# An mLSTM layer with top-1 experts: the last row blocks of three experts are made wider, and the group counts of the router are kept as running totals

## The chip, the cores and the metric

The kernel runs on one core of a Trainium2 chip. The metric is the time of one execution in microseconds (us) on the device, the median of several runs. TensorE does the matrix products (PE in the profile, and PEld for the loads of its stationary operand), VectorE (DVE) and ScalarE (ACT) the elementwise work, GpSimd (POOL) masks, products in SBUF and indirect transfers, and SyncE (SP) issues most transfers.

## The reference

Two parts follow each other. The first is a recurrence over 768 time steps for 4 batches and 8 heads of 40 numbers, with input, forget and output gates; its result is read as 3072 tokens of 320 numbers. The second sends every token to one of 8 experts.

```python
x = np.ascontiguousarray(attn_out.transpose(0, 2, 1, 3)).reshape(B * S, H * D)   # 3072 x 320
logits = x @ w_gate                                # 3072 x 8
expert_idx = np.argmax(logits, axis=1)
gate_w = probs[np.arange(N), expert_idx]           # probs: softmax of the logits
for e in range(E):
    mask = expert_idx == e
    h = np.maximum(x[mask] @ w1[e], 0.0)           # 320 -> 1024
    out[mask] = gate_w[mask, None] * (h @ w2[e])   # 1024 -> 320
```

How many tokens an expert gets is known only when the router has run.

## The kernel before

**First part, 24 items.** The recurrence is done in chunks of 128 steps: 6 chunks by 4 batches give 24 items of 128 tokens, and `step(s)` (L783) handles several items at different stages: `scores` (L282) and `pmul` (L289) of item s, `attend` (L305), `gated` and `state` of item s-1, `natural` (L345) and `finish` (L354) of item s-2. `finish` leaves the tokens' rows in `xs`, which `store` puts into `x_dram`, and the 8 logits of each token in `lg`. The program's order is the order of issue on every engine; no scheduler moves it.

**Routing, in 8 groups.** The items are routed in groups of 4, 4, 4, 2, 2, 4, 2 and 2 (`GROUPS`). `choose` (L383), on DVE two steps after the last item of the group, makes `oh`, a one-hot row of 8 for each token, and ends with a reduction over the group's items into `sums`, one 128x8 table a group (L401). `count` (L409), on PE one step later, adds up the place of each token in its expert's list in one PSUM tile, `pos`: a product with a triangular matrix `tri`, one product of a matrix of ones with `sums` of **each earlier group** (L415), one for each earlier item of the same group (L420), from item 14 on one with `less` and `gapb` (L425; `less` is a single row of -1, so this product has a contraction of one row), and one with the bases of the lists (L429). `place` turns this into slots, and `scatter` writes the tokens' numbers into lists in DRAM. `total` (L460) adds up `sums` over the groups so far, a product for each group, after items 12, 14 and 16 and once at the end, for the ranking of the experts.

**Second part, 10 pieces.** The experts are taken in the order of their counts, rank 0 to 7. Rank r has room for `CAPS[r]` rows, cut into blocks of at most 128 rows by `TILES[r]`; ranks 0 and 1 have 256 rows more, which are begun early as pieces a0 and a1, and their `TILES` are pieces b0 and b1. A piece has these steps: `load_list` (L545, SP) brings the list, one transfer for all blocks of the first block's size and a second for a last block that is smaller; `gather` (L561, POOL) fetches the rows, `norm` (L568, POOL) scales them; `third(k)` (L583), for the three thirds of the 320 columns, transposes each block on PE (L586: the block's rows are the contraction, so a block of 48 rows is a product with 48 rows of the array) and copies the result to SBUF on ACT and DVE. `first` (L593) multiplies with w1 for all rows of the piece at once, 8 chunks of 8 products, with ACT and DVE making `hh` and `hl` from each chunk. `second` (L612) multiplies with w2 block by block: 24 products of 320 columns a block, whose stationary operand has as many columns as the block has rows; ACT scales the result into `y`, and POOL writes the rows out by an indirect transfer (L627). The transposes of a piece stand in `second` of the piece before, `third(j)` ahead of block j. Both products use a high and a low part of weights and rows; a chunk of weights is made ready by a cast on ACT and a subtraction on DVE (`split`, L536).

`leftovers` (L637) calculates which experts have more tokens than their room; a loop at the end (L982) does them in blocks of 128. With these inputs the experts have 498, 464, 457, 422, 332, 329, 303 and 267 tokens, and no rank exceeds its room.

Of the kernel before, what the change touches and what calls it, by code (L numbers as in the profile page):

```python
# [13 lines left out]
BF16 = mybir.dt.bfloat16  # L14
# [3 lines left out]
ALU = mybir.AluOpType  # L18
AX = mybir.AxisListType

B, H, S, D = 4, 8, 768, 40
P = 128
# [8 lines left out]
E = 8  # L31
# [13 lines left out]
HEAD = HT * P  # L45
NPAIR = 2
FIRSTS = (P,) * HT
TILES = [(P,) * 2, (112,) * 2, (P, P, P, 80), (P, P, P, 48), (112,) * 3, (112,) * 3, (P, P, 64), (P, P, 32)]
CAPS = [sum(t) + HEAD * (r < NPAIR) for r, t in enumerate(TILES)]
FIRST, EARLY, MOST = 12, 14, 16  # L50
GROUPS = {
# [18 lines left out]
def mlstm_moe_kernel(ctx: ExitStack, tc: tile.TileContext, qk, og, kv, ig, fg, cst, tokid, lst0, w1, w2, out):  # L70
    nc = tc.nc
    PS = bass.MemoryType.PSUM
    const = ctx.enter_context(tc.tile_pool(name="const", bufs=1, side="left"))
# [20 lines left out]
    ones = const.tile([P, P], BF16, name="ones")  # L94
# [3 lines left out]
    oh = const.tile([P, NITEM, E], BF16, name="oh")  # L98
    sums = const.tile([P, len(GROUPS), E], BF16, name="sums")
# [4 lines left out]
    top = const.tile([P, 2, E], F32, name="top")  # L104
    big = const.tile([P, E], F32, name="big")
    gapb = const.tile([P, E], BF16, name="gapb")
    less = const.tile([1, P], BF16, name="less")
    ls0, ls1 = (const.tile([P, HT, 3], F32, name=f"ls{k}") for k in range(2))
    xg0, xg1 = (const.tile([P, HT, XR], F32, name=f"xg{k}") for k in range(2))
    xh0 = const.tile([P, 3, HEAD], F32R, name="xh0")  # L110
# [29 lines left out]
    at = list(spare)  # L140
# [239 lines left out]
    starts = [i0 for i0, _ in GROUPS.values()]  # L380
    group_of = starts.index

    def choose(i0, n):  # L383

        l3 = lg[:, i0 : i0 + n, :]
        b8 = lambda t: t.unsqueeze(2).to_broadcast([P, n, E])
        mx = mx_ps[:, :n]
        yield nc.vector.tensor_reduce(mx, l3, axis=AX.X, op=ALU.max)
        d = d_ps[:, : n * E].rearrange("p (n e) -> p n e", e=E)
        yield nc.vector.tensor_tensor(d, l3, b8(mx), ALU.subtract)  # L390
        rt["d", i0] = d

        sc = sm.tile([P, n, E], F32, name=f"sc{i0}", tag="sc")
        yield nc.vector.scalar_tensor_tensor(
            sc, d, 0.0, rev.unsqueeze(1).to_broadcast([P, n, E]), ALU.is_equal, ALU.mult
        )
        m2 = m2_ps[:, :n]
        yield nc.vector.tensor_reduce(m2, sc, axis=AX.X, op=ALU.max)
        yield nc.vector.tensor_tensor(oh[:, i0 : i0 + n, :], sc, b8(m2), ALU.is_equal)
        with nc.allow_low_precision("counts of at most four"):  # L400
            yield nc.vector.tensor_reduce(  # L401
                sums[:, group_of(i0)], oh[:, i0 : i0 + n, :].rearrange("p n e -> p e n"), axis=AX.X, op=ALU.add
            )

    def weights_of(i0, n):
# [3 lines left out]
    def count(i0, n):  # L409

        o3 = oh[:, i0 : i0 + n, :]
        rt["pos", i0] = pos = pos_ps[:, : n * E].rearrange("p (n e) -> p n e", e=E)
        nc.tensor.matmul(pos, tri, o3, start=True, stop=False, skip_group_check=True)
        for g in range(group_of(i0)):
            nc.tensor.matmul(  # L415
                pos, ones, sums[:, g].unsqueeze(1).to_broadcast([P, n, E]), start=False, stop=False,
                skip_group_check=True,
            )
        for j in range(n - 1):
            nc.tensor.matmul(  # L420
                pos[:, j + 1 :], ones, oh[:, i0 + j].unsqueeze(1).to_broadcast([P, n - 1 - j, E]), start=False,
                stop=False, skip_group_check=True,
            )
        if i0 >= EARLY:
            nc.tensor.matmul(  # L425
                pos, less, gapb[0:1].unsqueeze(1).to_broadcast([1, n, E]), start=False, stop=False,
                skip_group_check=True,
            )
        nc.tensor.matmul(pos, ones, baseb[:, :n], start=False, stop=True, skip_group_check=True)  # L429
# [30 lines left out]
    def total(items):  # L460

        rt["pc", items] = pc = pc_ps
        n = sum(i0 < items for i0 in starts)
        for g in range(n):
            nc.tensor.matmul(pc, ones, sums[:, g], start=g == 0, stop=g == n - 1)

    def rank(k, items):

# [225 lines left out]
    def start():  # L694
# [12 lines left out]
        for t, a, b in ((keep, 1.0, 0.0), (drop, 0.0, -1e30)):  # L707
# [3 lines left out]
        nc.gpsimd.affine_select(  # L711
            tri, ones, pattern=[[1, P]], compare_op=ALU.is_gt, fill=0.0, base=0, channel_multiplier=-1
        )
        nc.gpsimd.memset(less, -1.0)
        nc.gpsimd.memset(gapb, 0.0)
        nc.gpsimd.memset(zrow, 0.0)
        stir(8)
# [65 lines left out]
    def step(s):  # L783
# [44 lines left out]
        if chosen:  # L828
            weave(choose(*chosen))
# [36 lines left out]
    _, third = transpose_x("a0", xg0, FIRSTS)  # L866
    with tc.manual_schedule():
        start()
        for s in range(NITEM + 1):
            if s == 14:  # L870
# [21 lines left out]
        pieces = [(f"a{r}", r, 0, FIRSTS) for r in range(NPAIR)]  # L892
        pieces += [(f"b{r}", r, HEAD, TILES[r]) for r in range(NPAIR)]
        pieces += [(str(r), r, 0, TILES[r]) for r in range(NPAIR, E)]
        ls = {"a0": ls0, "a1": ls1}
# [6 lines left out]
        store(NITEM - 2)  # L902
        weave(finish(NITEM - 1))
        weave(choose(NITEM - 2, 2))
        weights_of(NITEM - 2, 2)
        store(NITEM - 1)
# [75 lines left out]
    with tc.For_i(0, nu) as u:  # L982
        e = nc.sync.value_load(tab[:, 0, ds(u, 1)], min_val=0, max_val=E - 1)
        at = nc.sync.value_load(tab[:, 1, ds(u, 1)], min_val=0, max_val=E * SS - P)
# [88 lines left out]
```

## Time and profile before

| | |
|---|---|
| median of 3 runs | 350.41 us (348.66, 350.41, 350.65) |
| profiled execution | 348.27 us, span 346.7 us |
| PE busy | 332.2 us (96%), 3370 products |
| DVE, ACT, POOL busy | 218.3, 190.6, 180.7 us |
| mean granted clock of TensorE | 0.975 |
| first part, with its routing | 0 to about 133 us |
| pieces a0 to b1 | about 133 to 202 us |
| ranks 2 to 7 | about 189 to 341.5 us |

The time of an execution is 1.6 us over its span. Products on PE overlap in their pipeline, so a row's duration is the time that one product takes from start to end (about 0.3 us), and the distance from one start to the next is what it costs in a dense stretch; a busy share of 96% therefore hides waits of less than about 0.2 us. The granted clock is 1.00 when TensorE has its full clock and 0.50 when it has half.

### The profile page before, as it was taken

To read this page: it belongs to the slowest core of one execution; us is meant where nothing else is said; L and a number is where in the kernel's file an instruction comes from. 1 tells how busy PE (TensorE), PEld (TensorE's weight loads), DVE (VectorE), ACT (ScalarE), POOL (GpSimd) and SP (SyncE) were. 2 spreads that over 40 slices of the span, in tenths; PEclk is the share of its full clock that TensorE was granted. 3 is DMA by queue.
4 is the path that set the end of the run, shared out by engine and by line. 5 is a ranking of instruction groups with operands and counts; after the bars stand their busy time and mean duration, and the time that the engine had idled before them with its cause. 6 is when DMAs were issued, how large, how long until landed. Compare 5 with 4: busy or idle time off the path is not lost. (4 is left out here: it accounts for less than half of the span.)

```text
span 346.7 us, 9329 instructions
## 1 busy us (share of the span) xinstructions
PE 332.2 (96%) x3370; PEld 307.7 (89%) x3370; DVE 218.3 (63%) x591; ACT 190.6 (55%) x477; POOL 180.7 (52%) x222
## 2 busy tenths in 40 slices
PE   7998999999999989998999999999999999999994
PEld 3797888999888768997999988999999999999992
DVE  5997888789789977854224758428427446374310
ACT  3989786777688732552325645336427445374311
POOL 7666597978986983317546661244145262222112
PEclk9899999999999965999999999999999999999999
DMA  6888888785989985548521874633654747630000
GB/s 168 254 253 243 265 229 202 210 234 140 247 196 233 275 183 140 153 48 250 155 70 42 254 190 115 206 115 110 194 146 120 205 130 219 172 92 22 27 19 23
DMA packets 33409, 56.75 MB, mean 164 GB/s; under 512 B 6296, under 2 KB 21437, under 8 KB 33346
## 3 DMA queue, kind: packets, MB, share of 16 engines
q1 hardware_dynamic: 29746, 47.88, 51.2%
q0 software_dynamic: 3424, 8.14, 7.8%
q8 instruction: 27, 0.44, 0.6%
q14 instruction: 20, 0.16, 0.2%
q10 hardware_dynamic: 192, 0.12, 0.1%
HBM read 48.12 MB, written 8.47 MB: 163 GB/s over the span
## 5 line engine op out<-in xcount | busy, mean ns | idle before, releaser
L622 PE MATMUL py<-w2h,hh 128*128 128x320 f32 (+5 forms) x224 | 71.3, 318 | 0.0
L622 PE MATMUL py<-w2h,hl 128*128 128x320 f32 (+5 forms) x224 | 69.0, 308 | 0.0
L622 PE MATMUL py<-w2l,hh 128*128 128x320 f32 (+5 forms) x224 | 69.0, 308 | 0.0
L627 POOL DMA_INDIRECT out<-y,ls x20 | 19.5, 973 | 94.6 <-ACT xh L587 57.9
L248 ACT ACTIVATE dd<-bc_ps,aT 128x128 f32<-128x128 f32 x184 | 51.0, 395 | 1.6 <-PE bc_ps L229 1.6
L607 DVE SCALAR_TENSOR_TENSOR hl<-bc_ps,hh 128x256 fp32r<-128x256 f32 (+6 forms) x54 | 25.6, 480 | 28.8 <-ACT hh L606 24.8
L622 PEld LDWEIGHTS py<-w2h,hh 128*128 128x128 f32 (+5 forms) x224 | 39.3, 176 | 1.0
L622 PEld LDWEIGHTS py<-w2l,hh 128*128 128x128 f32 (+5 forms) x224 | 39.3, 176 | 0.5
L622 PEld LDWEIGHTS py<-w2h,hl 128*128 128x128 f32 (+5 forms) x224 | 39.2, 175 | 0.6
L606 ACT ACTIVATE hh<-bc_ps 128x256 fp32r<-128x256 f32 (+6 forms) x54 | 23.4, 434 | 28.4 <-PE bc_ps L599 25.5
L626 ACT ACTIVATE y<-py,ls 128x320 f32<-128x320 f32 (+5 forms) x20 | 10.6, 528 | 49.6 <-issue 38.0
L257 POOL TENSOR_SCALAR_AFFINE_SELECT dd<-dd 128x1024 f32<-128x1024 f32 (+1 forms) x25 | 28.0, 1119 | 17.7 <-ACT dd L248 13.4
L599 PE MATMUL bc_ps<-xh,w1h 128*128 128x336 f32 (+5 forms) x114 | 36.7, 329 | 0.0
L599 PE MATMUL bc_ps<-xh,w1l 128*128 128x336 f32 (+5 forms) x114 | 36.4, 326 | 0.0
L534 DVE TENSOR_TENSOR w1l<-raw,w1h 128x1024 fp32r<-128x1024 f32 x24 | 30.7, 1280 | 6.9 <-ACT w1h L530 6.2
L452 POOL DMA_INDIRECT lst<-rec,slot x24 | 26.0, 1081 | 13.3 <-DVE r L362 4.3
L293 DVE TENSOR_TENSOR pp<-s_ps,dd 128x512 f32<-128x512 f32 x48 | 30.7, 679 | 0.3 <-issue 0.2
L287 PE MATMUL s_ps<-tq 40*128 40x128 f32 x384 | 29.7, 288 | 1.2 <-DVE pp L293 1.1
L563 POOL DMA_INDIRECT xg<-x_dram,ls x24 | 26.1, 1086 | 8.9 <-issue 5.2
L534 DVE TENSOR_TENSOR w2l<-raw,w2h 128x640 fp32r<-128x640 f32 x32 | 25.8, 821 | 7.5 <-ACT w2h L530 6.7
L349 PE MATMUL x_ps<-cs,yT 105*128 105x98 f32 x184 | 28.1, 298 | 2.6 <-ACT ex L407 1.9
L287 PEld LDWEIGHTS s_ps<-tq 40*128 40x128 f32 x384 | 24.5, 189 | 4.2 <-DVE pp L293 1.9
(223 smaller groups left out, 783.9 us busy)
## 6 DMA issues: line engine op xcount, KB each, us to landing
raw<-in_w SPq DMA_DIRECT2D x32, 320.0 KB
raw<-in_w SPq DMA_DIRECT2D x16, 512.0 KB
tk<-in_kv SPq DMA_DIRECT2D x24, 324.0 KB
tq<-in_qk SPq DMA_DIRECT2D x48, 160.0 KB
raw<-in_w SPq DMA_DIRECT2D x16, 256.0 KB
x_dram<-xs SPq DMA_DIRECT2D x24, 164.0 KB
og<-in_og SPq DMA_DIRECT2D x48, 80.0 KB
lst<-rec,slot POOLq DMA_INDIRECT x24
```

The lines of the kernel that those rows point to most:

```text
L248: nc.scalar.activation(dd[:, h, :], bc_ps[h // 4][:, (h % 4) * P : (h % 4 + 1) * P], AF.Exp, bias=aT[:, c, i : i + 1], scale=-1.0,)
L257: nc.gpsimd.affine_select(part, part, pattern=[[0, n], [1, P]], compare_op=ALU.is_ge, fill=0.0, base=0, channel_multiplier=-1)
L287: nc.tensor.matmul(s_ps[h // 4][:, p * P : (p + 1) * P], k, q, start=True, stop=True)
L293: nc.vector.tensor_mul(pp[:, 4 * k : 4 * k + 4], s_ps[k].rearrange("p (h t) -> p h t", t=P), t["dd"][:, 4 * k : 4 * k + 4])
L349: nc.tensor.matmul(x[:, o], t["yT"][:, o * P : (o + 1) * P], cs[:OR, C_R + o * XW : C_R + (o + 1) * XW], start=True, stop=True,)
L452: ins = nc.gpsimd.indirect_dma_start(out=lst, out_offset=bass.IndirectOffsetOnAxis(ap=slot[:, it : it + 1], axis=0), in_=rec[:, it, :], in ...
L534: nc.vector.tensor_sub(w[name + "l"][:, c], t, f32(w[name + "h"][:, c]))
L563: nc.gpsimd.indirect_dma_start(out=xg[:t, j], out_offset=None, in_=x_dram[: 1 + items * P], in_offset=bass.IndirectOffsetOnAxis(ap=ls[:t, ...
L599: nc.tensor.matmul(ph[:, :n], a[:, k, fs], b[:, k, :n], start=i == 0, stop=i == len(terms) - 1)
L606: nc.scalar.activation(hh[:, f, :n], ph[f][:, :n], AF.Relu)
L607: nc.vector.scalar_tensor_tensor(hl[:, f, :n], ph[f][:, :n], 0.0, f32(hh[:, f, :n]), ALU.max, ALU.subtract)
L622: nc.tensor.matmul(py[:t], a[:, f, ts], b[:, f], start=(f == 0 and i == 0), stop=(f == NF - 1 and i == 2))
```

## The change

Three of the rows of `TILES` are cut differently, with the same sums: rank 3 from (128, 128, 128, 48) to (112, 112, 112, 96), rank 6 from (128, 128, 64) to (112, 112, 96), rank 7 from (128, 128, 32) to (96, 96, 96). All three keep their number of blocks. `sums` of a group becomes the count over all items so far, so that `count` needs one product with `sums` of the group before and `total` one product in all; the reduction on DVE reads all items so far instead of the group's own. `less` becomes a full 128x128 matrix whose first row is -1 and whose others are 0, and is multiplied with all 128 rows of `gapb`.

```diff
-TILES = [(P,) * 2, (112,) * 2, (P, P, P, 80), (P, P, P, 48), (112,) * 3, (112,) * 3, (P, P, 64), (P, P, 32)]
+TILES = [
+    (P,) * 2, (112,) * 2, (P, P, P, 80), (112, 112, 112, 96), (112,) * 3, (112,) * 3, (112, 112, 96), (96,) * 3
+]
...
-    less = const.tile([1, P], BF16, name="less")
+    less = const.tile([P, P], BF16, name="less")
...
             yield nc.vector.tensor_reduce(
-                sums[:, group_of(i0)], oh[:, i0 : i0 + n, :].rearrange("p n e -> p e n"), axis=AX.X, op=ALU.add
+                sums[:, group_of(i0)], oh[:, : i0 + n, :].rearrange("p n e -> p e n"), axis=AX.X, op=ALU.add
             )
...
-        for g in range(group_of(i0)):
+        if i0:
+            before = sums[:, group_of(i0) - 1]
             nc.tensor.matmul(
-                pos, ones, sums[:, g].unsqueeze(1).to_broadcast([P, n, E]), start=False, stop=False,
-                skip_group_check=True,
+                pos, ones, before.unsqueeze(1).to_broadcast([P, n, E]), start=False, stop=False, skip_group_check=True
             )
...
-                pos, less, gapb[0:1].unsqueeze(1).to_broadcast([1, n, E]), start=False, stop=False,
+                pos, less, gapb.unsqueeze(1).to_broadcast([P, n, E]), start=False, stop=False,
...
-        n = sum(i0 < items for i0 in starts)
-        for g in range(n):
-            nc.tensor.matmul(pc, ones, sums[:, g], start=g == 0, stop=g == n - 1)
+        nc.tensor.matmul(pc, ones, sums[:, sum(i0 < items for i0 in starts) - 1], start=True, stop=True)
...
-        nc.gpsimd.memset(less, -1.0)
+        nc.gpsimd.memset(less, 0.0)
+        nc.gpsimd.memset(less[0:1], -1.0)
```

On PE, `count` and `total` of step 18 (items 14 and 15) stand like this before (a `LDWEIGHTS` row loads the stationary operand of the product behind it, and 128x16 is the product's output):

```order
L415 LDWEIGHTS ones
L415 MATMUL x_ps<-sums,ones 128x16
...
L420 LDWEIGHTS ones
L420 MATMUL x_ps<-oh,ones 128x8
L425 LDWEIGHTS less
L425 MATMUL x_ps<-gapb,less 128x16
L429 LDWEIGHTS ones
L429 MATMUL x_ps<-baseb,ones 128x16
L465 LDWEIGHTS ones
L465 MATMUL x_ps<-sums,ones 128x8
...
```

and like this in the change (line numbers are two or three higher):

```order
L418 LDWEIGHTS ones
L418 MATMUL x_ps<-sums,ones 128x16
L422 LDWEIGHTS ones
L422 MATMUL x_ps<-oh,ones 128x8
L427 LDWEIGHTS less
L427 MATMUL x_ps<-gapb,less 128x16
L431 LDWEIGHTS ones
L431 MATMUL x_ps<-baseb,ones 128x16
L465 LDWEIGHTS ones
L465 MATMUL x_ps<-sums,ones 128x8
```

Of four products at L415 one is left, and of five at L465 one. Over the program 21 and 16 products go, with their loads.

On PE, the transposes of rank 7 in `second` of rank 6, ahead of its first block, before:

```order
L599 MATMUL g_ps<-xh_4326,w1l_1528 128x320
L586 MATMUL s_ps_131<-cs,xg_4328 128x128 x2
L586 MATMUL s_ps_131<-cs,xg_4328 128x32
L622 MATMUL py_2693<-w2h_1529,hh 128x320
L622 MATMUL py_2693<-w2l_1530,hh 128x320
```

and in the change:

```order
L599 MATMUL g_ps<-xh_4289,w1l_1529 128x320
L586 MATMUL s_ps_131<-cs,xg_4291 128x96 x3
L622 MATMUL py_2670<-w2h_1530,hh 112x320
L622 MATMUL py_2670<-w2l_1531,hh 112x320
L622 MATMUL py_2670<-w2h_1530,hl 112x320
```

The number of transposes and products stays; their rows and the blocks' rows change. On SP the list of rank 7 was two transfers and is one, so that the weight transfers behind it stand one place further ahead:

```order
L552 DMA ls_2852<-lst 128x6
L552 ISA
L552 DMA ls_2852<-lst 32x3
L525 ISA
L525 DMA raw_2958<-in_w 128x1024
```

has become

```order
L552 DMA ls_2823<-lst 96x9
L525 ISA
L525 DMA raw_2928<-in_w 128x1024
```

where `raw` is the buffer into which a chunk of weights is loaded. Nothing else of SP's order moves.

## Rows read from the trace of the kernel before

**Rows 1.** Busy time by stretch (`PEclk`: granted clock); bounds in us from the span's start.
```profile
120.80:124.20 3.40, 3.40 (x22) 2.77 (x18) 3.17 (x4) 0.72 (x1) 2.94 (x4) 0.50 0.97 231
127.60:137.90 10.30, 9.81 (x52) 9.27 (x53) 7.19 (x29) 3.41 (x9) 5.50 (x10) 0.50 0.62 129
189.00:341.50 152.50, 152.11 (x999) 145.34 (x998) 79.78 (x138) 71.27 (x131) 51.30 (x54) 1.00 0.47 134
```

**Rows 2.** Waits of PE from 138 to 346 us: total, times, longest.
```profile
PE s_ps L586 <- POOL xgb L571: 0.6, 2, 0.3
```

**Rows 3.** Timeline of PE: transposes of a third, and the product behind them.
```profile
195.48 0.56 PE L586 MATMUL s_ps<-cs,xg 128*128 128x128 f32 x4
195.83 0.38 PE L622 MATMUL py<-w2h,hh 128*112 128x320 f32 x1
...
218.02 0.68 PE L586 MATMUL s_ps<-cs,xg 128*128 128x128 f32 x4
218.63 0.42 PE L622 MATMUL py<-w2h,hh 128*128 128x320 f32 x1
...
250.01 0.45 PE L586 MATMUL x_ps<-cs,xg 112*64 112x112 f32 x3
250.23 0.39 PE L622 MATMUL py<-w2h,hh 128*128 128x320 f32 x1
...
292.50 0.58 PE L586 MATMUL s_ps<-cs,xg 128*128 128x128 f32 x3
293.01 0.40 PE L622 MATMUL py<-w2h,hh 128*112 128x320 f32 x1
...
318.32 0.53 PE L586 MATMUL x_ps<-cs,xg 128*64 128x128 f32 x3
318.77 0.36 PE L622 MATMUL py<-w2h,hh 128*64 128x320 f32 x1
```

**Rows 4.** Timeline of PE's loads: the fourth transpose at 218 us.
```profile
218.44 0.14 PEld L586 LDWEIGHTS s_ps<-cs,xg 48*128 48x128 f32 x1 [0.17 <-issue]
```

**Rows 5.** Timeline of PE: the end of a count, and the last total.
```profile
97.30 0.17 PE L420 MATMUL x_ps<-oh,ones 128*128 128x8 bf16 x1
...
97.51 0.18 PE L429 MATMUL x_ps<-baseb,ones 128*128 128x16 bf16 x1
...
201.56 0.36 PE L465 MATMUL x_ps<-sums,ones 128*128 128x8 bf16 x8
201.77 0.46 PE L599 MATMUL bc_ps<-xh,w1h 128*128 128x464 f32 x1
```

**Rows 6.** DVE by line and form: the reduction into `sums`.
```profile
L401 DVE TENSOR_REDUCE sums<-oh 128x8 bf16<-128x32 bf16 x4 | 0.8, 206 | 0.1
L401 DVE TENSOR_REDUCE sums<-oh 128x8 bf16<-128x16 bf16 x4 | 0.7, 171 | 0.1
```

**Rows 7.** Timeline of DVE: the wait for it that ends at 118.1 us.
```profile
115.36 0.21 DVE L401 TENSOR_REDUCE sums<-oh 128x8 bf16<-128x32 bf16 x1
...
117.36 1.27 DVE L293 TENSOR_TENSOR pp<-s_ps,dd 128x512 f32<-128x512 f32 x2
```

**Rows 8.** Timeline of PE at that wait.
```profile
118.10 1.75 PE L287 MATMUL s_ps<-tq 40*128 40x128 f32 x16 [0.53 <-DVE pp L293]
```

**Rows 9.** Waits of PE from 20 to 133 us: those of scores for `pp`.
```profile
PE s_ps L287 <- DVE pp L293: 0.5, 1, 0.5
```

**Rows 10.** PE and PEld by line and form: products and loads of `second`.
```profile
L622 PE MATMUL py<-w2h,hl 128*128 128x320 f32 x128 | 39.4, 308 | 0.0
L622 PE MATMUL py<-w2h,hl 128*32 128x320 f32 x8 | 2.4, 306 | 0.0
...
L622 PEld LDWEIGHTS py<-w2h,hl 128*128 128x128 f32 x128 | 24.0, 188 | 0.0
L622 PEld LDWEIGHTS py<-w2h,hl 128*32 128x32 f32 x8 | 0.9, 108 | 0.3
```

**Rows 11.** The transfers out by tile: duration in ns, least, median, most.
```profile
L627 POOL DMA_INDIRECT out<-y,ls x20: 879/984/1033, 219.3 to 343.4; - x20
```

More of the change, by code (lines that the diff above doesn't have):

```diff
@@ L399, in choose @@
         yield nc.vector.tensor_tensor(oh[:, i0 : i0 + n, :], sc, b8(m2), ALU.is_equal)
-        with nc.allow_low_precision("counts of at most four"):
+        with nc.allow_low_precision("counts of at most 24"):
             yield nc.vector.tensor_reduce(
-                sums[:, group_of(i0)], oh[:, i0 : i0 + n, :].rearrange("p n e -> p e n"), axis=AX.X, op=ALU.add
+                sums[:, group_of(i0)], oh[:, : i0 + n, :].rearrange("p n e -> p e n"), axis=AX.X, op=ALU.add
             )
```

## The prediction

> **What bounds the kernel now.** I read the busy time by stretch first, then the waits of TensorE (PE), then its timeline where the change acts. From 189 us to 341.5 us PE is busy for 152.11 of 152.50 us at a granted clock of 1.00 [rows 1], and from 138 us to the end its longest kind of wait is 0.6 us, two pieces of 0.3 us, both for POOL's scaled rows at 160 us [rows 2]. So in ranks 2 to 7 the distance from one PE instruction to the next is the time itself, and what is taken out there moves the end. Ahead of 133 us it is mixed: PE waits now and then for DVE or ACT, as for 0.53 us at 118.10 us, for DVE's `pp` [rows 8]. Between 120.8 and 137.9 us the clock is at 0.50 for 3.4 and then 10.3 us [rows 1].
>
> **The transposes.** Rank 2 is cut into 128, 128, 128 and 80 rows, and its four transposes take 0.35 us from the first of them to the product behind them (195.48 to 195.83). Three of 112 rows take 0.22 us (250.01 to 250.23). Rank 3, with a last block of 48, takes 0.61 us (218.02 to 218.63); rank 6, with 64, takes 0.51 us (292.50 to 293.01); rank 7, with 32, takes 0.45 us in its last third (318.32 to 318.77) [rows 3]. The row of the loads shows where it goes: the load for the 48-row transpose, unlike those around it, begins only after 0.17 us in which nothing is loaded [rows 4], so it waits for the products in flight, and the product behind it then has to wait again. A block of 80 doesn't do this, so 96 and 112 shouldn't.
> There are three thirds a rank, hence nine such groups. Before: 3 x 0.61 + 3 x 0.51 + 3 x 0.45 = 4.71 us. After, by columns: rank 3 has 432 columns of transposes where rank 2 has 464, 0.35 x 432/464 = 0.33 us; rank 6 has 320 where three of 112 have 336, 0.21 us; rank 7 has 288, 0.19 us. That is 3 x (0.33 + 0.21 + 0.19) = 2.19 us. Saved: **2.5 us**, all of it between 213 and 319 us, in the stretch that has no waits. Least 0 (if the stop belonged to something else), most 2.8 us, if the stop also costs in the first product behind it.
> The 112x64 group at 250.01 us is one of third 2, where the output is only 64 rows wide, and it costs no more than 0.22 us [rows 3]: the stop comes from few rows of contraction, not from few columns. The Trainium skill, TensorEngine Tiling (Array Packing), section Key Properties, says that a change of the tiling mode drains the engine, and its Tiling Modes count 64 columns as a mode of their own. By that the three groups of third 2 would keep their stop and the saving would be about 1.7 us; the trace agrees for 48 and 64 rows and differs for 64 columns.
>
> **Products with wider blocks.** The last blocks go from 48, 64 and 32 columns of the stationary operand to 96. A product with 32 takes 306 ns and one with 128 takes 308 ns [rows 10]: 72 products x 2 ns = **+0.1 us**.
>
> **The end.** The last block written out has 96 rows and not 32. POOL's instruction takes between 0.88 us and 1.03 us over all sizes [rows 11], so at most +0.15 us; the transfer's own time for three times the rows stands in no row, and I bound it from 0 to 0.45 us, three times that spread. I take **+0.3 us** for both.
>
> **The counts.** Eight products with `sums` take 0.21 us (201.56 to 201.77), 0.026 us each. The product with `less` is different: from the product ahead of it to the one behind it pass 0.21 us (97.30 to 97.51) [rows 5], where two steps of the others make 0.05; with 128 rows it saves 0.16 us, four times. Removed products, by place: 3 in step 14, 5 in step 16, 7 in step 18 (with `less`), 4 in step 22 (with `less`), 5 in step 24 (with `less`), 6 in piece a0 (with `less`), 7 in the last total.
> Step 22's is lost: it stands right ahead of the wait at 118.10 us, which grows by what PE is early. Piece a0's is lost too: PE then waits at 160 us for rows that come through DVE and POOL [rows 2], which are no earlier. On the path remain 3 + 5 + 7 + 5 + 7 = 27 products x 0.026 = 0.70 us and 2 x 0.16 = 0.32 us: **-1.0 us**. At least 0.2 us (the last total alone, if the steps wait elsewhere), at most 1.6 us (37 x 0.026 + 4 x 0.16).
>
> **The longer reduction on DVE.** It reads 32, 64, 96, 112, 128, 160, 176 and 192 numbers where it read 32 or 16. From 16 to 32 it grows from 171 to 206 ns [rows 6], 2.2 ns a number, so the eight get longer by 0, 0.07, 0.14, 0.21, 0.25, 0.28, 0.35 and 0.39 us. Those up to step 17 delay a `pp` that stands behind them on DVE, but in the whole first part PE's scores wait for `pp` once only, at 118 us [rows 9]; without that cover they would cost 0.67 us. Step 23's lies ahead of an idle time of DVE, and a0's likewise; without these, 0.74 us. Step 21's is bare: at 115.36 us it stands ahead of a weight chunk and of the `pp` at 117.36 us [rows 7], for which PE waits at 118.10 us [rows 8]. **+0.3 us**, from 0 to 1.7 us.
>
> **What I put at nothing.** The second memset of `less` (one of 128 rows and one of one row, for one before) lies on POOL ahead of its first mask, which waits for ACT. One list transfer fewer lets the weight transfers behind it on SP start earlier; PE waits for no weights in these rows, and it would matter only if they were late. POOL's gathers and scalings keep their number and their columns.
>
> **Sum.** -2.5 + 0.1 + 0.3 - 1.0 + 0.3 = **-2.8 us**. Against the profiled execution: 348.27 - 2.8 = 345.5 us. The median shown is 350.41 us, 2.1 us above that execution; one of its runs lies at 348.66 and two at 350.4 to 350.7. With the median as the base: **347.6 us**.
>
> **Rivals.**
> (a) Only part of it arrives: third 2 keeps its stop, or the steps before 113 us give nothing because they end on ACT and DVE. For it speaks that PE waits there for others in some steps; against it the 112x64 group, and that its scores wait once only [rows 9]. Gain 0.8 to 2.0 us, 348.4 to 349.6 us. Chance 0.17.
> (b) The clock, which ends slower. PE's wait at 118.10 us grows to 0.53 + 0.26 + 0.28 = 1.07 us, just ahead of the stretch at 0.50 from 120.8 us [rows 1]. Each further 3.4 us at half clock of dense products loses 1.7 us. One leaves a gain of 1.1 us; from the second on the change loses, 2 x 1.7 - 2.8 = +0.6 us, 351.0 us; four give 354.4 us. Against it: behind 137.9 us PE has its products back to back, and from 189 us the clock stays at 1.00 [rows 1]. One: chance 0.05; two or more: 0.04.
> (c) The clock the other way: with the shifted steps a half-clock stretch of 3.4 us is missing, a further -1.7 us, 345.9 us or less. Nothing in the rows favours it over (b) but its order of size. Chance 0.06.
> (d) The wider loads show. A load of 32 columns takes 108 ns and one of 128 takes 188 ns [rows 10], 0.83 ns a column; 24 loads x 144 columns more x 0.83 = 2.9 us, which would eat all of the transposes' gain: 350.5 us. Against it: the products with 128 columns, whose loads are longer than any of the new ones, take 308 ns like those with 32 take 306. The Trainium skill, TensorE: Matmul & The Clock Gate, section LDWEIGHTS, has a load's time grow with its columns and not with its rows, which speaks against this change; the trace agrees on the load and shows it hidden. Chance 0.02.
> (e) The change doesn't do what it says: blocks of 96 or 112 stop as well, so that only the counts remain, 350.0 us. The 80-row block speaks against it. Chance 0.02.
> The forecast itself, a gain of 2.0 to 3.6 us: 0.64.
>
> **How the numbers follow.** The forecast's own range is 346.8 to 348.4 us on the median's base. An execution like the profiled one would lie 2.1 us lower, at 344.7 to 346.3 us, and two of the four times shown are of that kind; so the range starts at 345.2 us. Upward it takes in (a) and ends at 349.6 us; outside remain most of (b), (d), (e) and a low execution with the full gain, together under 0.2. A measurement of this kernel tells about 1% from no change, 3.5 us. Faster by that means under 346.9 us: the forecast's range straddles that bound once the lower executions are counted, and I give it half of 0.64 less a little, 0.31; with (c) 0.37. Slower by over 1% is (b) from some four stretches on; I leave it the whole 0.04. Within 1%: 0.59.
>
> **What would show it.** Each of the nine groups of transposes in ranks 3, 6 and 7 at 0.19 to 0.36 us; no load with 0.17 us of idle time before it there. Counts with products 0.026 us apart through `less`. The reduction at 0.4 to 0.56 us in the last groups, and PE's wait near 118 us at about 1 us. From 213 to 319 us the stretch shorter by 2.5 us, and the tail behind the last product longer by 0.3 us. The prediction is wrong if these hold and the time doesn't follow, which would put the loss into 97 to 160 us, or if a group with 96 rows takes over 0.4 us.

## The result, and the profile after

The changed kernel takes 345.94 us (median of 6 runs, 345.02 to 348.10), the kernel before beside it 350.48 us (6 runs, 348.66 to 351.10): a ratio of 0.9885, 95% interval 0.9848 to 0.9922. Two later comparisons gave 0.9869 (0.9832 to 0.9905; 345.35 against 349.08 us) and 0.9954 (0.9910 to 0.9997; 345.06 against 347.62 us). The three differences of the medians are 4.5, 3.7 and 2.6 us; the prediction had 2.8 us. The medians are over all executions and the ratios leave out those that ran long, so the one does not divide into the other; by the ratios the gains are 4.0, 4.6 and 1.6 us.

The profiled execution of the changed kernel is the slowest of its six (348.10 us), that of the kernel before (348.27 us) is faster than every one of the six that stand beside the changed kernel. The two spans, 346.5 and 346.7 us, therefore don't show the difference; it has to be looked for stretch by stretch. In the stretch in which PE is busy throughout, by the columns of [rows 1]:

```profile
189.00:341.50 152.50, 151.43 (x1011) 148.41 (x1009) 81.20 (x139) 73.42 (x136) 52.61 (x56) 1.00 0.47 134
```

The granted clock is 1.00 and PE is busy for 151.43 of 152.50 us; the end of that window now reaches into the tail. The first transpose of rank 2 starts at 193.63 us, the last product of all at 340.48 us: 146.85 us, where before they were at 191.53 and 341.15 us, 149.62 us. So 2.77 us have gone between two points with the same work between them.

The timeline of PE, a third of ranks 3, 6 and 7 each as in [rows 3], the third one being third 2 with its 64-row output:

```profile
215.72 0.54 PE L586 MATMUL s_ps<-cs,xg 112*128 112x112 f32 x4
216.04 0.39 PE L622 MATMUL py<-w2h,hh 128*128 128x320 f32 x1
...
223.56 0.54 PE L586 MATMUL x_ps<-cs,xg 112*64 112x112 f32 x4
223.88 0.39 PE L622 MATMUL py<-w2h,hh 128*128 128x320 f32 x1
...
289.38 0.44 PE L586 MATMUL s_ps<-cs,xg 112*128 112x112 f32 x3
289.60 0.39 PE L622 MATMUL py<-w2h,hh 128*112 128x320 f32 x1
...
317.77 0.41 PE L586 MATMUL x_ps<-cs,xg 96*64 96x96 f32 x3
317.97 0.36 PE L622 MATMUL py<-w2h,hh 128*96 128x320 f32 x1
```

From the first transpose to the product behind it: 0.32 us three times in rank 3, 0.22 us three times in rank 6, 0.19 to 0.20 us three times in rank 7, 2.21 us in all. Before, the nine were 0.60, 0.61, 0.58, 0.51, 0.51, 0.49, 0.49, 0.49 and 0.45 us, 4.73 us: **2.52 us less**. And the loads of rank 3's transposes are one row without a gap, where [rows 4] had 0.17 us ahead of the fourth:

```profile
215.51 0.55 PEld L586 LDWEIGHTS s_ps<-cs,xg 112*128 112x128 f32 x4
216.01 0.19 PEld L622 LDWEIGHTS py<-w2h,hh 128*128 128x128 f32 x1
```

The last total is one product now, and the next product of `first` starts 0.03 us behind it instead of 0.21 us [rows 5]:

```profile
203.66 0.18 PE L465 MATMUL x_ps<-sums,ones 128*128 128x8 bf16 x1
203.69 0.45 PE L599 MATMUL bc_ps<-xh,w1h 128*128 128x464 f32 x1
```

That is 0.18 us, and with the transposes 2.70 of the 2.77 us.

The count of step 22, and the scores of step 23 behind it: the product with `less` (L427) takes its place in the pitch of 0.03 us, without the stop that [rows 5] showed, and PE then waits for `pp` as in [rows 8]:

```profile
119.33 0.22 PE L422 MATMUL x_ps<-oh,ones 128*128 128x24 bf16 x3
119.40 0.18 PE L427 MATMUL x_ps<-gapb,less 128*128 128x32 bf16 x1
119.43 0.18 PE L431 MATMUL x_ps<-baseb,ones 128*128 128x32 bf16 x1
120.27 0.48 PE L289 MATMUL s_ps<-tq 40*128 40x128 f32 x2 [0.67 <-DVE pp L295]
```

On DVE, the longer reduction with 160 and with 192 numbers, where [rows 6] had 171 and 206 ns for the group's own:

```profile
118.05 0.43 DVE L403 TENSOR_REDUCE sums<-oh 128x8 bf16<-128x160 bf16 x1
118.40 1.21 DVE L534 TENSOR_TENSOR w1l<-raw,w1h 128x1024 fp32r<-128x1024 f32 x1
119.54 1.28 DVE L295 TENSOR_TENSOR pp<-s_ps,dd 128x512 f32<-128x512 f32 x2
...
137.98 0.49 DVE L403 TENSOR_REDUCE sums<-oh 128x8 bf16<-128x192 bf16 x1
```

A wait that had not been there shows in the view of PE's waits from 138 to 346 us. Before, the longest single one in that view was of 0.6 us, the first of these lines, which [rows 2] doesn't have; the others are those of the changed kernel:

```profile
PE bc_ps L599 <- issue: 0.6, 1, 0.6
...
PE bc_ps L599 <- DVE sums L403: 2.2, 1, 2.2
PE bc_ps L599 <- issue: 0.8, 1, 0.8
PE bc_ps L599 <- DVE hl L607: 0.4, 1, 0.4
```

Piece a0's products ran at full clock here and came to the end of the chain of choices on DVE, which the reduction at 137.98 us closes, before DVE did. The wait ends at 138.96 us, and from 140.5 us the granted clock is 0.50 for 3.4 us, in dense products:

```profile
140.50:143.90 3.40, 3.40 (x22) 3.31 (x21) 2.01 (x6) 0.79 (x4) 0.72 (x1) 0.50 0.45 100
```

Two further profiles of the same kernel ("again" and "once more" below) have half clock ahead of this place, from 130.5 us on, and don't have this wait.

The end: POOL's instruction for the last transfer out, which took 0.88 us at 343.43 us before.

```profile
342.85 0.92 POOL L627 DMA_INDIRECT out<-y,ls  x1 [3.54 <-issue]
```

From the last product's start to POOL's instruction 2.37 us (before 341.15 to 343.43, 2.28 us), from there to the end of the span 3.63 us (before 3.23 us): the tail is 6.0 us and was 5.5 us.

What hides all this in the two spans lies in front. The scores of step 3 (the fourth of 24; the expectations below call them those of step 4, and those of step 23, the last, those of step 24):

```profile
21.91 1.16 PE L289 MATMUL s_ps<-tq 40*128 40x128 f32 x16
```

In the profiled execution before they started at 20.00 us. The half clock of the start lay at 17.6 to 21.0 us here and at 11.6 to 15.0 us there. The kernel before, profiled once more (last experiment), had these scores at 22.7 us, behind half clock from 11.1 to 21.4 us: the difference goes with the execution, not with the change.

### The profile page after: what moved, and what is told of

Same layout as the page of the kernel before. It is cut to its first block, busy times and chain, and to the rows that moved or that the text cites. A ratio compares the mean times of both kernels' runs of the same rounds, so it can differ in the third digit from the quotient of the medians.

```text
span 346.5 us, 9253 instructions
## 1 busy us (share of the span) xinstructions
PE 327.5 (95%) x3333; PEld 305.4 (88%) x3333; DVE 219.3 (63%) x591; ACT 189.9 (55%) x477; POOL 178.7 (52%) x223
## 5 line engine op out<-in xcount | busy, mean ns | idle before, releaser
L622 PE MATMUL py<-w2h,hh 128*112 128x320 f32 (+3 forms) x224 | 71.1, 317 | 0.0
L622 PE MATMUL py<-w2h,hl 128*112 128x320 f32 (+3 forms) x224 | 69.1, 308 | 0.0
L622 PE MATMUL py<-w2l,hh 128*112 128x320 f32 (+3 forms) x224 | 69.1, 308 | 0.0
L622 PEld LDWEIGHTS py<-w2l,hh 128*112 128x112 f32 (+3 forms) x224 | 39.3, 176 | 0.0
L622 PEld LDWEIGHTS py<-w2h,hh 128*112 128x112 f32 (+3 forms) x224 | 39.3, 175 | 0.0
L622 PEld LDWEIGHTS py<-w2h,hl 128*112 128x112 f32 (+3 forms) x224 | 39.2, 175 | 0.0
L259 POOL TENSOR_SCALAR_AFFINE_SELECT dd<-dd 128x1024 f32<-128x1024 f32 (+1 forms) x25 | 26.8, 1073 | 21.5 <-ACT dd L250 13.3
L626 ACT ACTIVATE y<-py,ls 112x320 f32<-112x320 f32 (+3 forms) x20 | 10.5, 527 | 47.2 <-issue 35.8
L534 DVE TENSOR_TENSOR w1l<-raw,w1h 128x1024 fp32r<-128x1024 f32 x24 | 29.5, 1231 | 7.3 <-ACT w1h L530 7.2
```

Of the source, the lines that this page charges most:

```text
L259: nc.gpsimd.affine_select(part, part, pattern=[[0, n], [1, P]], compare_op=ALU.is_ge, fill=0.0, base=0, channel_multiplier=-1)
L534: nc.vector.tensor_sub(w[name + "l"][:, c], t, f32(w[name + "h"][:, c]))
L622: nc.tensor.matmul(py[:t], a[:, f, ts], b[:, f], start=(f == 0 and i == 0), stop=(f == NF - 1 and i == 2))
```

## The experiments

My theory: PE stops where a transpose contracts over 64 rows or fewer, these nine stops are the gain, and what the counts save is small. Against it: the counts and `less`, which free PE in the part with the routing, are most of it; that the stop belongs to something else than the rows; and that the longer reduction gives the counts' gain back.

**The cut of the ranks alone.**

```diff
-TILES = [(P,) * 2, (112,) * 2, (P, P, P, 80), (P, P, P, 48), (112,) * 3, (112,) * 3, (P, P, 64), (P, P, 32)]
+TILES = [
+    (P,) * 2, (112,) * 2, (P, P, P, 80), (112, 112, 112, 96), (112,) * 3, (112,) * 3, (112, 112, 96), (96,) * 3
+]
```

> The kernel before with the new block sizes alone. Theory A (the stop at transposes of 64 rows or fewer): the nine groups of transposes in ranks 3, 6 and 7 at 0.19 to 0.33 us, 2.6 us less in all, the tail 0.3 to 0.5 us longer, so 2.2 us faster than before. Theory B (most of the 4.5 us comes from the counts): the groups shrink, but the time falls by under 1.5 us.

Measured 346.21 us against 349.08 us, ratio 0.9893 (0.9854 to 0.9932). Groups of 0.32, 0.22 and 0.19 us; rank 2's transposes to the last product 147.0 us, tail 6.0 us. That is 2.9 us by the medians, where 2.2 us were expected; the cut alone brings most of the change.

**The running totals alone**, `less` left with one row.

```diff
-                sums[:, group_of(i0)], oh[:, i0 : i0 + n, :].rearrange("p n e -> p e n"), axis=AX.X, op=ALU.add
+                sums[:, group_of(i0)], oh[:, : i0 + n, :].rearrange("p n e -> p e n"), axis=AX.X, op=ALU.add
...
-        for g in range(group_of(i0)):
+        if i0:
...
```

> The kernel before with the running totals alone; the row of -1 keeps its one row. Theory A: 37 products fewer, 0.7 us of them on the path, the longer reductions cost 0.3 us, so 0.4 us faster (0 to 1). Theory B: 2 us or more faster, from the first part up to 160 us.

Measured 348.01 us, ratio 0.9964 (0.9931 to 0.9997). Transposes as before; rank 2's transposes to the last product 149.4 us, so 0.2 us less, the last total. The interval allows from 0.1 to 2.4 us, which excludes neither expectation.

**The full `less` alone.**

```diff
-    less = const.tile([1, P], BF16, name="less")
+    less = const.tile([P, P], BF16, name="less")
...
-                pos, less, gapb[0:1].unsqueeze(1).to_broadcast([1, n, E]), start=False, stop=False,
+                pos, less, gapb.unsqueeze(1).to_broadcast([P, n, E]), start=False, stop=False,
```

> The kernel before with the full matrix in place of the row of -1 alone. Theory A: four products follow the one before them after 0.03 us and not 0.10 us, two of them on the path, so 0.3 us faster (0 to 0.6). Theory B: 1 us or more faster, since the first part waits less behind it.

Measured 348.75 us, ratio 0.9978 (0.9952 to 1.0005): it can't be told from no change, though a gain of up to 1.7 us is not excluded. 149.6 us from rank 2's transposes to the last product.

**The changed kernel again**, beside these three.

> The changed kernel once more, for a second profile and beside the parts. Theory A: 4 to 5 us faster than before as measured, with the transposes' stretch 2.7 us shorter as in the first profile and the rest gained ahead of 190 us, where the first profile had lost 2 us by 22 us from the start. Theory B: the same time, with the gain ahead of 190 us larger than the one behind it.

Measured 345.35 us, ratio 0.9869: 3.7 us by the medians, a little under the expected 4 to 5 us. The three parts add up to 1.07 + 0.36 + 0.22 = 1.65% against 1.31% for the whole, each to some 0.35%: they add up as far as can be told. The profile (345.18 us) has the same kind of start as the first one of before (scores of step 3 at 20.0 us) and is 3.1 us shorter than that, with 146.85 us behind rank 2's first transposes.

**Last blocks of 72 rows.** Is it the bound at 64, or something finer?

```diff
-TILES = [
-    (P,) * 2, (112,) * 2, (P, P, P, 80), (112, 112, 112, 96), (112,) * 3, (112,) * 3, (112, 112, 96), (96,) * 3
-]
+TILES = [(P,) * 2, (112,) * 2, (P, P, P, 80), (120, 120, 120, 72), (112,) * 3, (112,) * 3, (124, 124, 72), (108, 108, 72)]
```

> The changed kernel with the last blocks of ranks 3, 6 and 7 at 72 rows (120, 120, 120, 72; 124, 124, 72; 108, 108, 72) in place of 96. Theory A (only blocks of 64 rows or fewer stop TensorE): the nine groups of transposes take 0.20 to 0.33 us each, 2.2 us in all, and the time is that of the changed kernel within 0.3%. Rival (rows that are no multiple of 16 or 32 stop it as well, or the bound lies above 72): groups of 0.45 to 0.6 us, 4.7 us in all, and a time about 2.4 us longer than the changed kernel's.

The groups take 0.34, 0.24 and 0.22 us, 2.39 us in all (some 0.02 us each over the changed kernel's), and rank 2's transposes to the last product 147.0 us. No stop at 72 rows, though 72, 108, 120 and 124 are no multiples of 16. Measured 344.85 us against 347.56 us, ratio 0.9930 (0.9874 to 0.9986), within the spread of the changed kernel's three ratios; the changed kernel was not timed beside it. Here is rank 6's third 0:

```profile
284.02 0.44 PE L584 MATMUL s_ps<-cs,xg 124*128 124x124 f32 x3
284.26 0.38 PE L620 MATMUL py<-w2h,hh 128*112 128x320 f32 x1
```

**The old blocks, with 128 rows of contraction.** The blocks of 48, 64 and 32 rows come back, but are turned by a product with the identity's first columns over all 128 rows, the rows beyond the block zeroed by POOL.

```diff
-                nc.tensor.transpose(pt[:r, at : at + t], xg[:t, j, k * P : k * P + r], ident[:t, :t])
+                if t > 64:
+                    nc.tensor.transpose(pt[:r, at : at + t], xg[:t, j, k * P : k * P + r], ident[:t, :t])
+                else:
+                    nc.tensor.matmul(
+                        pt[:r, at : at + t], xg[:, j, k * P : k * P + r], ident[:, :t], start=True, stop=True
+                    )
...
+                if t <= 64:
+                    nc.gpsimd.memset(xg[key][t // 64 * 64 :, j, :DM], 0.0)
```

> The changed kernel with the old blocks of 48, 64 and 32 rows, but each of these transposed by a product over all 128 rows of contraction (rows beyond the block are zeroed, the right operand is the identity's first 48, 64 or 32 columns). Theory A (the stop comes from few rows of contraction): no stop, the nine groups take 0.20 to 0.36 us each, 2.3 us in all, and the tail behind the last product is 5.5 us and not 6.0: 0.3 to 0.6 us faster than the changed kernel. Rival (the stop comes from the narrow output, 32 to 64 columns): the groups keep 0.45 to 0.6 us, 4.7 us in all, and the time is about 2 us longer than the changed kernel's.

Measured 346.93 us against 347.56 us, ratio 0.9982 (0.9931 to 1.0034), an interval too wide to decide between the two expectations. The profile (an execution of 356.56 us) shows that neither holds as it stands; its clock is at 1.00 in the rows below. First rank 3's third 0, its loads and then its products (L587 is the new one; in single precision it comes as two):

```profile
222.57 0.46 PEld L585 LDWEIGHTS s_ps<-cs,xg 128*128 128x128 f32 x3
223.00 0.30 PEld L587 LDWEIGHTS s_ps<-cs,xg 128*128 128x128 f32 x2
223.22 0.19 PEld L625 LDWEIGHTS py<-w2h,hh 128*128 128x128 f32 x1
```

```profile
222.78 0.49 PE L585 MATMUL s_ps<-cs,xg 128*128 128x128 f32 x3
223.11 0.32 PE L587 MATMUL s_ps<-cs,xg 128*128 128x48 f32 x2
223.25 0.39 PE L625 MATMUL py<-w2h,hh 128*128 128x320 f32 x1
```

No gap in the loads, and 0.47 us for the group (0.36 us in ranks 6 and 7): with the same 48 columns of output, and 128 rows, the stop is gone, in thirds 0 and 1 of all three ranks. What remains over the changed kernel's 0.32 us goes with the two loads of 128 columns for one block. In rank 3's third 2, whose stationary operand has 64 columns, the stop is there again:

```profile
230.78 0.36 PEld L585 LDWEIGHTS x_ps<-cs,xg 128*64 128x64 f32 x3
231.34 0.19 PEld L587 LDWEIGHTS x_ps<-cs,xg 128*64 128x64 f32 x2 [0.20 <-issue]
231.58 0.19 PEld L625 LDWEIGHTS py<-w2h,hh 128*128 128x128 f32 x1
```

0.66, 0.57 and 0.54 us for these three groups. The nine sum to 4.15 us, nearer to the rival's 4.7 than to the theory's 2.3: 0.58 us are saved where the cut saves 2.52, and the tail is the old one, 5.5 us. I had not thought of third 2 as a case of its own. (This profile has half clock from 16.0 to 29.7 and from 36.5 to 50.1 us, and no time is read from its first part.)

**The short reduction, with the total added on POOL.**

```diff
-                sums[:, group_of(i0)], oh[:, : i0 + n, :].rearrange("p n e -> p e n"), axis=AX.X, op=ALU.add
+                sums[:, group_of(i0)], oh[:, i0 : i0 + n, :].rearrange("p n e -> p e n"), axis=AX.X, op=ALU.add
...
+    def running(i0, n):
+        if i0:
+            own = sums[:, group_of(i0)]
+            with nc.allow_low_precision("counts of at most 24"):
+                nc.gpsimd.tensor_add(own, own, sums[:, group_of(i0) - 1])
...
```

> The changed kernel with the reduction on DVE cut back to the group's own rows (16 or 32 numbers, 0.17 to 0.21 us) and the total of the groups before added by POOL at the end of the step. Theory (the longer reduction is what eats the counts' gain): PE's wait for pp at 118 to 120 us goes from 0.67 to 0.4 us or less, piece a0's wait for sums gets shorter by 0.3 us if POOL's addition lies aside, and the time is 0.3 to 0.7 us shorter than the changed kernel's. Rival (the counts' gain is lost because the steps end on ACT and DVE anyhow): the step starts from 30 to 118 us stay where they are within 0.3 us and the time is the changed kernel's within 0.1%.

Both expectations fell: 352.19 us against 347.56 us, ratio 1.0178 (1.0091 to 1.0265). The addition takes 0.2 us on POOL but stands behind its masks and list transfers, and PE waits for it:

```profile
PE x_ps L471 <- POOL sums L411: 2.6, 3, 1.4
```

The longest, 1.40 us, ends at 100.57 us, and the granted clock is 0.50 from 102.0 to 115.7 us, a place where no other profile has half clock:

```profile
102.00:115.70 13.70, 13.70 (x146) 11.89 (x142) 8.49 (x31) 6.86 (x20) 9.00 (x12) 0.50 0.89 245
```

13.7 us of dense products at half clock lose some 6.8 us, by an estimate from this row; the scores of step 23 come 94.5 us behind those of step 5, 5 to 9 us later than in the table below. The stretch behind rank 2's transposes is the changed kernel's, 146.8 us. So what the prediction's rival (b) feared, half clock soon behind a wait, does occur in this kernel. The changed kernel itself has it too: in its first profile half clock begins at 140.5 us, 1.5 us behind the end of the wait of 2.22 us, and in the profile "once more" below at 116.9 us, inside a wait of 3.09 us. It does not always follow: in the profiles with the full `less` alone and with the cut alone waits of 2.38 and 1.52 us, which end at 161.64 and 160.04 us, have no half clock behind them.

**Each reduction twice.** If the longer reduction were what eats the counts' gain, doubling it would show.

```diff
-            yield nc.vector.tensor_reduce(
-                sums[:, group_of(i0)], oh[:, : i0 + n, :].rearrange("p n e -> p e n"), axis=AX.X, op=ALU.add
-            )
+            for _ in range(2):
+                yield nc.vector.tensor_reduce(
+                    sums[:, group_of(i0)], oh[:, : i0 + n, :].rearrange("p n e -> p e n"), axis=AX.X, op=ALU.add
+                )
```

> The changed kernel with each reduction into the totals of the groups done twice in a row on DVE (the same values): 0.20 + 0.27 + 0.33 + 0.36 + 0.38 + 0.43 + 0.47 + 0.49 = 2.9 us more of DVE. Theory (DVE's time in the first part is covered but for step 21's and piece a0's reductions): PE's wait for pp at 118 to 120 us grows from 0.67 to about 1.1 us, piece a0 starts up to 0.5 us later, and the time is 0.4 to 1.0 us longer than the changed kernel's. Rival (DVE's time is the bound of steps 14 to 24, and the longer reduction is what ate the counts' gain): the scores of step 24 come 2 us later or more, seen from those of step 5, and the time is 2 to 3 us longer.

Measured 346.37 us, ratio 0.9942 (0.9898 to 0.9987), beside the changed kernel's 345.06 us, 0.9954 (0.9910 to 0.9997). From the scores of step 5 to those of step 23 it needs 87.2 us, no more than the others (table below), and the wait at 118 us is

```profile
118.39 1.75 PE L289 MATMUL s_ps<-tq 40*128 40x128 f32 x16 [0.80 <-DVE pp L295]
```

0.80 us and not 1.1. The median is 1.3 us over the changed kernel's and the ratio 0.1% below its own, so 2.9 us more on DVE cost nothing that can be told; the rival, whose scores would come 2 us later, fell.

**The change without its running totals** (the new cut, the full `less`, a product for each group and the short reduction).

Against the kernel before:

```diff
-TILES = [(P,) * 2, (112,) * 2, (P, P, P, 80), (P, P, P, 48), (112,) * 3, (112,) * 3, (P, P, 64), (P, P, 32)]
+TILES = [
+    (P,) * 2, (112,) * 2, (P, P, P, 80), (112, 112, 112, 96), (112,) * 3, (112,) * 3, (112, 112, 96), (96,) * 3
+]
...
-                pos, less, gapb[0:1].unsqueeze(1).to_broadcast([1, n, E]), start=False, stop=False,
+                pos, less, gapb.unsqueeze(1).to_broadcast([P, n, E]), start=False, stop=False,
...
```

> The kernel before with the new cut of the ranks and the less operand of 128 rows, but a product for each group and the short reduction: the change without its running totals. If the running totals give what the prediction's terms give (34 products of 0.026 us of which 27 lie on the path, against 0.3 us of DVE), it is 0.4 us slower than the changed kernel; if the longer reduction costs more than the products, it is faster by up to 1 us. By the sum of the parts measured so far 0.3% slower.

Measured 345.37 us, ratio 0.9952 (0.9917 to 0.9987): 0.3 us over the changed kernel, less than can be told. Rank 2's transposes to the last product 147.0 us.

**The changed kernel once more**, on the same chip as the last two.

> The changed kernel again, on the same chip as the two others, to compare them with: a ratio to the kernel before of 0.985 to 0.992.

0.9954 is above the expected 0.985 to 0.992, and the upper end of its interval, 0.9997, all but reaches no change. The gain in the time is known only as 0.5 to 1.3%. Its profile (342.92 us) has a wait that shows what the first part waits for:

```profile
117.56 0.79 PE L289 MATMUL s_ps<-tq 40*128 40x128 f32 x2 [3.09 <-DVE pp L295]
```

```profile
112.71 0.45 DVE L403 TENSOR_REDUCE sums<-oh 128x8 bf16<-128x160 bf16 x1
113.07 3.83 DVE L534 TENSOR_TENSOR w1l<-raw,w1h 128x1024 fp32r<-128x1024 f32 x1
116.83 1.27 DVE L295 TENSOR_TENSOR pp<-s_ps,dd 128x512 f32<-128x512 f32 x2
```

PE had come to this place early: the last product of the count starts 84.9 us behind step 5's scores (114.29 - 29.4), in the first profile of this kernel 87.8 us (119.43 - 31.6). 2.9 us had been gained on the way, and the wait is 2.4 us longer. The weight chunk ahead of `pp` stood on DVE for 3.83 us. The chunks are cast on ACT and subtracted on DVE in the same order, and the cast of this one had run from 108.87 to 109.98 us, so it was not waiting for that. What lies beside it are products of two operands on POOL (L271 and L571; the masks of L259 have one):

```profile
112.88 1.27 POOL L271 TENSOR_TENSOR qg<-tq,gb 104x512 f32<-104x512 f32 x1
...
115.76 2.40 POOL L571 TENSOR_TENSOR xg<-xg 128x320 f32<-128x320 f32 x2
```

The same place in the first profile of the kernel before, where such a product of POOL runs until 116.35 us:

```profile
115.48 1.96 DVE L534 TENSOR_TENSOR w1l<-raw,w1h 128x1024 fp32r<-128x1024 f32 x1
```

All profiles but the padded kernel's show it for the three chunks of `w1l` from 102 to 130 us: 1.21 to 1.28 us where at most 0.2 us of a chunk lies beside such a product, 1.3 to 1.6 us beside 0.24 to 0.56 us, 2.0 to 2.1 us beside 0.87 to 1.05 us, and 3.83 us here, beside 2.22 us. That the product on POOL is what holds DVE up fits all of them; no run here varies it by itself.

**The kernel before, profiled once more.**

> The kernel before, once more, for a second profiled execution: scores of step 4 at 20.0 us or at 21.6 to 21.9 us from the span's start, whichever of the two kinds of start it has; if the later one, the span is 1.6 to 1.9 us longer than the first profiled execution's, and the stretch from rank 2's first transposes to the last product's start is 149.6 us either way.

349.13 us (one execution), span 347.5 us, scores of step 3 at 22.7 us (neither of the two values I had named), and 149.6 us between the two points. Its time is 0.9 us over the first profile's though it starts 2.7 us later, so the start does not decide alone either.

The profiles, in us from their timelines (the half clock is the time at a granted clock of 0.50 from 113 to 189 us). The padded and the POOL kernel, with half clock between 30 and 113 us, are not among them:

| profile | step 5's scores | to step 23's | to rank 2's transposes | to the last product | tail | half clock |
|---|---|---|---|---|---|---|
| before | 29.7 | 88.4 | 73.4 | 149.6 | 5.5 | 13.7 |
| before, once more | 32.5 | 86.9 | 73.1 | 149.6 | 5.5 | 10.2 |
| full `less` | 31.3 | 88.3 | 73.9 | 149.6 | 5.5 | 17.1 |
| running totals | 31.4 | 88.3 | 73.5 | 149.4 | 5.5 | 13.7 |
| cut alone | 29.7 | 89.1 | 73.1 | 147.0 | 6.0 | 10.2 |
| cut and `less` | 31.2 | 86.0 | 74.7 | 147.0 | 6.0 | 20.5 |
| after | 31.6 | 88.6 | 73.4 | 146.8 | 6.0 | 6.8 |
| after, again | 29.7 | 88.2 | 72.8 | 146.8 | 6.0 | 10.2 |
| after, once more | 29.4 | 88.2 | 70.8 | 146.9 | 6.0 | 10.2 |
| 72 rows | 31.3 | 85.9 | 71.1 | 147.0 | 6.0 | 13.7 |
| reduction twice | 31.2 | 87.2 | 73.5 | 146.9 | 6.0 | 13.7 |

The two columns behind rank 2 are the same to 0.2 us in every execution of a kind. Those ahead of it spread by 2.8 and 2.6 us over four executions that run almost the same instructions there: "72 rows" differs from "after", "after, again" and "after, once more" only from the list of rank 3 on, which SP loads behind 150 us.

## Why the prediction was right, and where it was not

The forecast of -2.8 us lies inside the three measured differences of 2.6 to 4.5 us, and 345.94 us inside its own range. What the profiles can place is -2.5 us for the transposes, -0.2 us for the last total and +0.5 us for the tail, -2.2 us in all; what the medians show beyond that isn't placed. That the forecast lies among the measured differences is in part luck: it has 0.8 us more gain from the counts than the profiles place, and the measured gain holds something that neither the forecast nor the profiles place. By its steps:

- **Transposes, -2.5 us: right**, in size (-2.52 us) and in mechanism. No stop at 72 rows or more, stops at 48, 64 and 32; the same 48, 64 and 32 columns of output with 128 rows of contraction don't stop where 128 columns are loaded. So for transposes few rows of contraction make it, as the prediction read it from the 80-row block [rows 3].
- **64 columns.** The prediction weighed a sentence of the Trainium skill, TensorEngine Tiling (Array Packing), Key Properties, that a change of the tiling mode drains the engine, against the 112x64 group, and took the row. For transposes the runs bear that out: third 2 of ranks 3, 6 and 7 takes 0.32, 0.22 and 0.20 us. But the product over 128 rows with 64 columns, in the padded kernel, does stop by 0.20 us. That stop fits the sentence of the Trainium skill only if the transposes with 64 columns right ahead of it are not in the mode for 64 columns, since from one product with 64 columns to the next no mode would change. The products of `second` with 48 and 32 columns of the kernel before do not stop either: they follow those with 128 at 0.14 us (253.68 to 253.82 us, 337.71 to 337.85 us). The runs leave open what parts these three; the padded product is the only one that shows as two products.
- **Wider blocks, +0.1 us: nothing seen.** 309 ns for a product with 96 columns, 306 ns with 32 [rows 10], but the distance from one to the next, which is what counts here, is 0.15 us with either. The longer loads of the last blocks stay hidden, 161 ns in place of 108. Rival (d) had a fault of its own: its 2.9 us counted the 144 columns that the last blocks gain and not the 144 that the other blocks lose (3 x 16, 2 x 16 and 2 x 32), so that at 0.83 ns a column it comes to nothing even if no load is hidden.
- **The end, +0.3 us: too small by 0.2 us**, inside its bounds. 0.13 of the 0.5 us lie ahead of the last transfer's issue and in it, the rest in the transfer.
- **The counts, -1.0 us: mis-sized; the profiles place 0.2 us of it.** The rows came as said: no stop at `less`, a pitch of 0.03 us. The last total gave 0.18 us. The step that failed is the claim that 27 of the products remain on the path, which rested on PE's scores waiting for `pp` only once [rows 9]. The steps wait for more than `pp`: in the profile after, from 20 to 133 us, PE waits 1.3 us for `yT`, 0.7 us for DVE's L485 and 0.6 us for ACT's exponentials, and these waits come and go between executions of the same instructions. What the counts free in a step is within that; the running totals and `less` alone show 0.4% and 0.2%, with intervals that reach to 0.03% and beyond nothing. Against the change without its running totals the whole change gains 0.3 us by the medians and nothing by the ratios. A gain of the predicted size can't be excluded by these runs; it isn't shown either.
- **The longer reduction, +0.3 us: nearer to nothing.** It takes 0.20 to 0.49 us, 1.8 ns a number and not 2.2. The wait at 118 us was said to become 1.07 us; in the changed kernel it was 0.67, 0.67 and 3.09 us; with the long reduction in the kernels of 72 rows and of the totals alone 0.32 and 0.49 us, with it doubled 0.80 us, with the short one 0.53, 0.82 (full `less`) and 0.47 us (cut and `less`), and under 0.2 us in two more. The step that failed is that step 21's reduction is "bare". The weight chunk behind it took 1.96 us before (it stands where [rows 7] have "..."), partly beside a product of POOL; in the changed kernel, with the reduction 0.2 us longer, it begins behind that product and takes 1.21 us (118.40 us). Over all profiles with the short reduction it took 1.21 to 2.00 us, so that a step's end there follows the chunk and its neighbour on POOL more than the reduction. a0's reduction was put at nothing and cost nothing: it ends at 138.47 us, ahead of the wait's end at 138.96 us, but ACT's `hh`, which DVE's `hl` behind it also needs, ends at 138.45 us and does not depend on it.
- **The clock, rival (b).** Half clock from 113 to 189 us is 6.8 to 13.7 us in the four profiles with the change's counts and cut, 10.2 and 13.7 us in the two of before. So the total is not larger with the change. In its first profile one stretch of 3.4 us begins 1.5 us behind a wait that was not there before; whether the wait brought it is not shown. The POOL version shows what rival (b) costs where it comes: all six of its executions have a mean granted clock of 0.950 to 0.960, where those of the changed kernel lie at 0.955 to 0.990.
- **The base.** The prediction put the median's 2.1 us over the profiled execution down as given. The table shows where such differences lie: in the part ahead of rank 2, with its start, its waits and its half-clock stretches. The prediction had also read the longest kind of wait behind 138 us as POOL's scaled rows; a single wait of 0.6 us, without a releaser that the profile shows, stood beside them.

## What to carry to other kernels

In a stretch where TensorE is busy throughout at full clock, cut the rows so that no transpose contracts over 64 rows or fewer between full ones: each such transpose cost 0.26 to 0.29 us here, and the saving was the same in every execution. Instructions saved on TensorE in a part that waits for other engines and for weights need not move the end: the same products were worth their full price at 203 us and nothing that could be measured at 60 to 118 us. Moving 0.2 us of work to an engine that is half idle can make a kernel slower by some 5 us (352.19 us against 347.56 us for the kernel before) when it stands in that engine's queue and TensorE waits for it.

## What the runs showed of the hardware

- A transpose over 48, 64 or 32 rows between full ones: 0.17 to 0.20 us without a load, and 0.26 to 0.29 us longer for the group than with the changed cut; over 72, 96, 108, 112, 120 or 124 rows nothing.
- A product with one row of contraction, in a row of full ones 0.03 us apart, took 0.21 us from the product ahead of it to the one behind it where 128 rows take 0.05 us: filling the other 127 rows with zeros is cheaper than leaving them out.
- A subtraction of 128x1024 single-precision numbers on VectorE took 1.21 to 1.28 us with at most 0.2 us of a two-operand product on GpSimd beside it, 1.96 us beside 0.87 us and 3.83 us beside 2.22 us.
- The half clock of the start lies at 11.6 to 15.0 us in one execution of the kernel before and at 11.1 to 21.4 us in another, and the scores of step 3 follow at 20.0 and 22.7 us; in the first profile of the changed kernel it lies at 17.6 to 21.0 us, with these scores at 21.9 us.
- With almost the same instructions (the four executions named under the table), the part from step 5 to rank 2's transposes took 156.9 to 162.0 us.
